# Moving the attention transposes and value products one unit later in a fused attention, MLP and expert kernel

## The chip, the cores and the metric

The kernel runs on one core of a Trainium2 chip. The metric is the device time of one execution in microseconds (us); several runs are given by their median. TensorE is called PE here, VectorE DVE, ScalarE ACT, GpSimd POOL and SyncE SP, as in the profile.

## The reference

Three stages follow one another, all in float32:

```python
# 1. attention: q, k, v are (4, 8, 576, 64); M_prev (4, 8, 64, 64), z_prev (4, 8, 64), beta (8)
scores = np.matmul(q, k.transpose(0, 1, 3, 2)) / np.sqrt(D)        # causal mask, softmax over keys
local = np.matmul(softmax(scores), v)
q_p = phi(q)                                                        # x > 0: x + 1, else exp(x)
mem_out = einsum('bhsd,bhde->bhse', q_p, M_prev) / (einsum('bhsd,bhd->bhs', q_p, z_prev)[..., None] + 1e-06)
x = g * mem_out + (1 - g) * local                                   # g = sigmoid(beta), per head
# 2. MLP on 2304 tokens of 512: w_in (512, 2048), w_out (2048, 512)
x = relu(x @ w_in) ** 2 @ w_out
# 3. one expert of eight for each token, by cosine similarity: w1 (8, 512, 1024), w2 (8, 1024, 512)
out = gate * (relu(x @ w1[e]) @ w2[e])
```

## The kernel before

**Units.** Two heads make a pair; there are 16 pairs, four to each of the four batches. A pair has nine units, in the order `ORDER`: first `(None, 4)`, the last 64 rows of both heads at once, and then a head (0 or 1) and a block r of 128 rows: (0, 3), (1, 3), (0, 0), (1, 0), (0, 2), (1, 2), (0, 1), (1, 1). The main loop of `attention` counts steps `t`; in step `t` the scores of unit `t` are issued, so that pair `p` begins at step `9p`. Within a pair the step is called `i` here (0 to 8).

**A unit's way through the engines.** In its step PE multiplies (`scores`, L437) into a bank of PSUM. One step later DVE adds the mask, copies and finds the row maximum (L441), and ACT takes the exponential (L447). Two steps later, once both heads of a block are there, DVE forms the reciprocal sums (L455, L456) and POOL scales (`scale`): in the first batch a diagonal matrix (L395), in later batches the matrix `A` itself (L398), for both heads together with the second one. `LT = 4` steps after the scores PE transposes (`turn`, L403, or L405 with the diagonal), into two PSUM banks of the tag T. In the step after that ACT copies the transposes out (L575), and `LP = 7` steps after the scores PE multiplies by the values (`values`, L531) and, once a pair, by `M_prev` (L510, L534).

**Preparation of the next pair.** The generator `prep(p + 1)` begins in pair `p` at step `i = START` (3 for the first pair, 2 for the second, 1 afterwards) and takes one stage a step. It transposes k (`tk`, L294) and q (`tq`, L300), splits each into a high and a low part (ACT L295, L301; DVE L296, L302), moves halves with DMAs (`moves`, L290), transposes the 64 last rows of both (`t2`, L324, L325) and splits them too (`tail_hi` on ACT L328, L331; `tail_lo` on DVE L334, L337). It also forms phi(q) (ACT L321, DVE L344, L345), weighs it with z_prev (POOL L348), sums (DVE L353) and normalises (POOL L361); these results are transposed last (`tp`, `t3`). The scores of the next pair's `(None, 4)` read the split tails. `kn` and `qn`, which take k and q, are single buffers.

**Loads.** `load(p + 2)` issues all inputs of a pair on SP's queue: three DMAs each for k, q and v, two for M_prev and one for z_prev, at step `START + 5`.

**The MLP in between.** From step 44 on, `step` gives half a step of the MLP to each step of the loop but `i = REST = 4`: either twelve matmuls of its first layer (L681) or six of its second (L715 to L717). While it has begun only what the finished batches allow, `batches = (t - 8) // 36` sets the limit. Its weights must be split into high and low parts before, and this conversion is spread over steps 5 to 64 (`CONV`: 27 stages by step 43, 51 by step 64). A piece of weights is loaded into one of two `raw` tiles, and passes ACT (L132), DVE (L134 to L139), ACT (L141) and POOL (L143). Two pieces are under way at once (`conversions2`); the next piece's load is issued in the first of the three stages of each round, which is also the stage in which DVE reads the older piece's `raw` tile for the last time (L139).

**Order.** PE runs in the order of the program throughout. Up to step 8 ACT, DVE and POOL do too; later their order, and that of SP's queue at all times, comes from a planner that works with its own estimates of costs and dependencies. Every engine runs its list in order.

Of the kernel before, what the change touches and what calls it, by code (L numbers as in the profile page):

```python
# [14 lines left out]
ALU = mybir.AluOpType  # L15
# [9 lines left out]
NPP = H // 2  # L25
NPAIR = B * NPP
# [22 lines left out]

LT, LP = 4, 7
WT = 2
NA, NAS = 3, 4
XD = 4
# [102 lines left out]
def conversions2(*args):  # L158


    old = iter(())
    new = conversion(*args[:4], 0, *args[4:])
    next(new)
    for n in range(1, 18):
        for k in range(3):
            next(old, None)
            next(new, None)
            if k == 0 and n < 16:
                ahead = conversion(*args[:4], n, *args[4:])
                next(ahead)  # L170
            yield
        old, new = new, ahead if n < 16 else iter(())


def attention(tc, sh, q, k, v, M, z, beta, w_in, w_out, mlp, step):

    nc = tc.nc
    with ExitStack() as ctx:
# [36 lines left out]
        def later(d, eng, f):  # L215
            queue.setdefault((now[0] + d, eng), []).append(f)

        def load(p):
            b, hp = divmod(p, NPP)
            vn = vns[p % 3]  # L220
            zb = st.tile([128, 128], F32, name="zb", tag="zb")
            Mt = Mts[p % 3]
            for src, t in ((k, kn), (q, qn), (v, vn)):
                eng = nc.scalar if p == 0 and src is q else nc.sync
                for h in range(2):
                    eng.dma_start(t[:, 0:4, h * 64:h * 64 + 64],
                                      src[b, 2 * hp + h, 0:512].rearrange("(c p) d -> p c d", p=128))
                eng.dma_start(t[:64, 4].rearrange("p (h d) -> p h d", h=2),
                                  src[b, 2 * hp:2 * hp + 2, 512:576].rearrange("h p d -> p h d"))
            for h in range(2):  # L230
                hs = slice(h * 64, h * 64 + 64)
                nc.sync.dma_start(Mt[hs, hs], M[b, 2 * hp + h])
            nc.sync.dma_start(zb, z[b:b + 1, 2 * hp:2 * hp + 2].rearrange("o h d -> o (h d)").to_broadcast([128, 128]))
            nat[p] = (vn, zb, Mt)

        load(0)
        warm = c.tile([128, 1], F32, name="warm")
        nc.scalar.activation(warm, ident[:, 0:1], AF.Exp)
        g_all = c.tile([128, H], F32, name="g_all")
# [33 lines left out]
        def prep(p):  # L273
# [46 lines left out]

            later(1, "act", lambda: nc.scalar.activation(e, qn, AF.Exp))  # L321
            yield
            t2 = new_T(p, "t2")
            nc.tensor.transpose(t2[:, 0:64], kn[:64, 4], ident[:64, :64])  # L324
            nc.tensor.transpose(t2[:, 64:128], qn[:64, 4], ident[:64, :64])  # L325
# [13 lines left out]

            later(1, "act0", tail_hi)  # L340
            later(1, "dve0", tail_lo)

            def phi():
                nc.vector.tensor_scalar_min(e, e, 1.0)  # L344
                nc.vector.scalar_tensor_tensor(e, qn, 0.0, e, ALU.max, ALU.add)  # L345

            later(1, "dve", phi)
            later(1, "pool", lambda: nc.gpsimd.tensor_tensor(u, e, zb.unsqueeze(1).to_broadcast([128, 5, 128]), ALU.mult))  # L348
            for _ in range(2 if p else 4):
                yield  # L350

            def norm():
# [209 lines left out]
        while t < len(units) + LP + 5 or queue:  # L562
            now[0] = t
            p, i = divmod(t, 9)
            if t == STRICT:
                strict.close()
            if t in BUSY:
                busy(BUSY[t])
            if t == 1:
                load(1)  # L570
            start = START[min(p, 2)]
            if 0 <= p < NPAIR - 1 and i == start:
                gens.append(prep(p + 1))
            for d, x in evacs:
                nc.scalar.copy(d, x)  # L575
            evacs.clear()
            due("act0")
            if before is not None:
                next(before)
            if here is not None:  # L580
                next(here)
            due("dve0")
            if here is not None:
                next(here)
            before, here = here, None
            if t == MIX:
                mix()
            due("act")
            due("dve")
            due("pool")  # L590
            while sh.converted < int(by(CONV, t)):
                next(conv, None)
                sh.converted += 1
            if 0 <= t - LP < len(units):
                values(*units[t - LP])
            if 0 <= p < NPAIR - 2 and i == start + 5:
                load(p + 2)
            if t % 9 != REST:
                step(t)
            for g in list(gens):  # L600
                if next(g, gens) is gens:
                    gens.remove(g)
            if 0 <= t - LT < len(units):
                turn(*units[t - LT])
            if 0 <= t < len(units):
                here = scores(*units[t])
                next(here)
            t += 1
# [743 lines left out]
@with_exitstack  # L1352
def tile_kernel(ctx, tc, q, k, v, M, z, beta, w_in, w_out, emb, tau, w1, w2, out):
    nc = tc.nc
    sh = Shared()
    sh.R = None
    sh.const = ctx.enter_context(tc.tile_pool(name="const", bufs=1))
    big = ctx.enter_context(tc.tile_pool(name="big", bufs=1))
    dr = ctx.enter_context(tc.tile_pool(name="dr", bufs=1, space=DRAM))
    sh.x2p = dr.tile([NT, DM], F32, name="x2p")  # L1360
    sh.x2d = dr.tile([NT, DM], F32, name="x2d")
    sh.end = dr.tile([E, DM], F32, name="end")
    sh.ident = sh.const.tile([128, 128], F32, name="ident")
    make_identity(nc, sh.ident)
    sh.Wh = [[big.tile([128, 1024], F32R, name=f"Wh0_{j}") for j in range(8)]]
    sh.Wl = [[big.tile([128, 1024], F32R, name=f"Wl0_{j}") for j in range(8)]]
    sh.room = ctx.enter_context(tc.tile_pool(name="room", bufs=1))
    sh.x1 = {j: big.tile([128, 4, CH], F32, name=f"x1_{j}") for j in range(NCH - 2)}
    psm = ctx.enter_context(tc.tile_pool(name="psm", bufs=2, space=PSUM))
    with ExitStack() as mctx:  # L1370
        mlp = Mlp(mctx, psm, tc, sh, w1, w2)

        sh.converted, sh.begun = 0, False

        def step(t):


            batches = (t - 8) // (9 * NPP)
            if sh.begun:
                mlp.second()  # L1380
            elif mlp.at < 48 and ((mlp.at + 1) // 8 + 1) * CH <= batches * S and min(6 * mlp.at + 9, 51) <= sh.converted:
                mlp.square = nc.scalar if mlp.at < 16 else nc.vector
                mlp.first()
            else:
                return
            sh.begun = not sh.begun

        with tc.manual_schedule(engines={ENG.PE}):
            attention(tc, sh, q, k, v, M, z, beta, w_in, w_out, mlp, step)
        mlp.later = at_once  # L1390
        mlp.square = nc.scalar
        mlp.psr = sh.psr = ctx.enter_context(tc.tile_pool(name="psr", bufs=1, space=PSUM))
        mlp.room = {NCH - 3: 3, NCH - 2: 7}
        big2 = ctx.enter_context(tc.tile_pool(name="big2", bufs=1, side="right", reuse_waits="tile"))
        sh.Wh.append([big2.tile([128, 1024], F32R, name=f"Wh1_{j}") for j in range(8)])
        sh.Wl.append([big2.tile([128, 1024], F32R, name=f"Wl1_{j}") for j in range(8)])
        with ExitStack() as cctx:
            st = cctx.enter_context(tc.tile_pool(name="cst", bufs=2))
            conv = conversions(nc, st, sh, 1, nc.vector, w_in, w_out)
            done = 0  # L1400
            while mlp.steps[mlp.at][0] == 0:
                mlp.advance()
                done += CONV2
                while done >= 1:
                    next(conv, None)
                    done -= 1
            for _ in conv:
                pass
            for _ in range(mlp.LAG):
                mlp.advance()  # L1410
        mlp.square = nc.scalar
        routing_setup(tc, sh, ctx.enter_context(tc.tile_pool(name="rp", bufs=1, side="right", reuse_waits="tile")))
        sh.R.ps = ctx.enter_context(tc.tile_pool(name="prr", bufs=1, space=PSUM, side="right", reuse_waits="tile"))
        mlp.routing(sh.rpool, mctx.enter_context(tc.tile_pool(name="late", bufs=2, reuse_waits="tile")), emb, tau)
        while mlp.advance():
            pass
        for _ in sh.R.first:
            pass
    gates = tables(ctx, tc, sh)
    next(gates)  # L1420
    experts(tc, sh, gates, w1, w2, out)
# [31 lines left out]
```

## Time and profile before

| | |
|---|---|
| median of 3 runs | 965.38 us (962.93 to 967.06) |
| the profiled execution: its time | 968.15 us |
| the profiled execution: its span | 966.4 us |
| PE busy over the span | 914.8 us |
| pairs 8 to 15 of the attention, each | about 24.2 us |
| end of the attention's loop | about 411 us |

The span runs from the first to the last instruction; the time holds 1.75 us more around it. A pair is measured from the first matmul of its `(None, 4)` scores to that of the next pair. Pair 1 begins at 31.21 us, pair 2 at 55.40, pair 3 at 73.48, pair 4 at 97.88, pair 5 at 118.10, pair 6 at 146.48, pair 7 at 174.56 and pair 8 at 201.22. In a row of a timeline the first number is the start, the second the duration, and a bracket holds the idle time of the engine before it with what ended it.

### The profile page before, as it was taken

The numbers are of one execution on the slowest core, as the hardware profiler recorded it, in microseconds if no ns is written. First come the engines' busy times: TensorE is split into PE (matmuls) and PEld (weight loads), VectorE is DVE, ScalarE is ACT, GpSimd is POOL, SyncE is SP. The second block draws the span as 40 slices with busy tenths as digits, with TensorE's granted clock in tenths as the row PEclk, the third lists the DMA queues.
The fourth block names the chain that finished last, engine by engine and source line by source line (L and its number), as shares of the span: only waits on it lengthen the run. The fifth ranks groups of instructions, "written<-read, shape, count | busy, mean of one in ns | idle before, by whom it ended". The sixth has DMA issues, their size and how long they took to land.

```text
span 966.4 us, 19224 instructions
## 1 busy us (share of the span) xinstructions
PE 914.8 (95%) x6271; PEld 792.3 (82%) x6271; DVE 604.4 (63%) x1745; ACT 526.2 (54%) x1355; POOL 281.5 (29%) x353
## 2 busy tenths in 40 slices
PE   7987888899999999999999999999999999999993
PEld 6765766688888888899888888888899899989983
DVE  4886677656666665488616778889772535353661
ACT  3676677677666766577645555655421424242440
POOL 4453555533333443100211111333310311111111
PEclk8999999899999999999999999999999999999997
DMA  7676555454444440155220111521160634353521
GB/s 162 141 181 154 141 157 134 102 124 95 119 97 119 95 99 1 66 154 167 89 73 23 55 63 69 198 66 45 34 219 14 198 104 155 114 168 94 173 82 34
DMA packets 107081, 105.79 MB, mean 109 GB/s; under 512 B 66096, under 2 KB 76336, under 8 KB 106945
## 3 DMA queue, kind: packets, MB, share of 16 engines
q1 hardware_dynamic: 101200, 90.17, 33.6%
q0 software_dynamic: 4544, 13.67, 4.5%
q8 instruction: 65, 1.06, 0.5%
q14 instruction: 72, 0.58, 0.2%
q10 hardware_dynamic: 1200, 0.30, 0.2%
HBM read 70.80 MB, written 14.70 MB: 88 GB/s over the span
## 4 chain that ended last, share of the span: by engine, by line
PE 74%; issue 5%; DVE 3%; POOL 1%; ACT 0%; POOLq 0%; DVEq 0%
PE ps L681 20%; PE psh L1248 11%; PE y L715 7%; PE y L717 6%; PE y L716 6%; PE psy L1266 3%; PE psy L1264 3%; PE psy L1265 3%; PE xo L531 3%; PE ps L437 3%; PE pt L403 3%; DVE x L818 1%; PE xo L510 1%; PE pst L964 1%; POOL out_dram L1329 0%
## 5 line engine op out<-in xcount | busy, mean ns | idle before, releaser
L681 PE MATMUL ps<-xh,Wh 128*128 128x256 f32 x416 | 120.1, 289 | 0.0
L681 PE MATMUL ps<-xl,Wh 128*128 128x256 f32 x416 | 118.2, 284 | 1.0 <-DVE xl L655 1.0
L681 PE MATMUL ps<-xh,Wl 128*128 128x256 f32 x416 | 118.1, 284 | 0.0
L447 ACT ACTIVATE A<-A,nm 128x576 f32<-128x576 f32 (+2 forms) x144 | 84.4, 586 | 59.7 <-DVE nm L441 40.5
L715 PE MATMUL y<-Wh,gh 128*128 128x512 f32 x288 | 115.3, 400 | 0.0
L717 PE MATMUL y<-Wh,gl 128*128 128x512 f32 x288 | 113.7, 395 | 0.1
L716 PE MATMUL y<-Wl,gh 128*128 128x512 f32 x288 | 113.4, 394 | 0.0
L398 POOL TENSOR_SCALAR A<-A,sm,g 128x512 f32<-128x512 f32 (+4 forms) x108 | 74.1, 694 | 119.4 <-DVE sm L456 77.7
L1250 ACT ACTIVATE hh<-psh 128x512 fp32r<-128x512 f32 x44 | 26.4, 599 | 147.3 <-PE psh L1248 76.4
L1248 PE MATMUL psh<-xTh,Wh 128*128 128x256 f32 x352 | 100.1, 284 | 2.0 <-issue 1.3
L691 DVE TENSOR_TENSOR gl<-r,gh 128x256 fp32r<-128x256 f32 x144 | 73.8, 514 | 42.3 <-ACT gh L690 38.4
L1248 PE MATMUL psh<-xTh,Wl 128*128 128x256 f32 x352 | 99.5, 283 | 0.2 <-DVE Wl L111 0.2
L1248 PE MATMUL psh<-xTl,Wh 128*128 128x256 f32 x352 | 99.3, 282 | 0.0
L685 ACT ACTIVATE r<-ps 128x256 f32<-128x256 f32 x144 | 54.6, 379 | 74.2 <-PE ps L681 64.7
L441 DVE CUSTOM_DVE_ANT_0 A<-ps,mask 128x256 f32<-128x256 f32 (+4 forms) x160 | 75.6, 479 | 26.6 <-PE ps L437 24.7
L1251 DVE SCALAR_TENSOR_TENSOR hl<-psh,hh 128x512 fp32r<-128x512 f32 x44 | 30.4, 690 | 94.9 <-ACTq L1238 38.1
L681 PEld LDWEIGHTS ps<-xh,Wh 128*128 128x128 f32 x416 | 79.8, 192 | 4.7 <-issue 1.9
L681 PEld LDWEIGHTS ps<-xl,Wh 128*128 128x128 f32 x416 | 79.9, 192 | 3.8 <-DVE xl L655 1.2
L681 PEld LDWEIGHTS ps<-xh,Wl 128*128 128x128 f32 x416 | 79.9, 192 | 0.0
L690 ACT CAST gh<-r 128x256 fp32r<-128x256 f32 x144 | 58.4, 405 | 38.3 <-PE y L716 35.4
L1248 PEld LDWEIGHTS psh<-xTh,Wh 128*128 128x128 f32 x352 | 66.9, 190 | 4.0 <-issue 2.1
L1248 PEld LDWEIGHTS psh<-xTl,Wh 128*128 128x128 f32 x352 | 66.8, 190 | 0.7
(328 smaller groups left out, 2416.2 us busy)
## 6 DMA issues: line engine op xcount, KB each, us to landing
x<-in_moe_w_dram SPq DMA_DIRECT2D x48, 512.0 KB, 8.8
raw<-in_moe_w_in_dram SPq DMA_DIRECT2D x16, 512.0 KB, 4.7
raw<-in_moe_w_out_dram SPq DMA_DIRECT2D x16, 512.0 KB, 3.8
ks<-hk SPq DMA_DIRECT2D x60, 128.0 KB, 2.5
x2d<-x SPq DMA_DIRECT2D x18, 256.0 KB, 2.0
kn<-in_k_dram SPq DMA_DIRECT2D x32, 128.0 KB, 4.2
vn<-in_v_dram SPq DMA_DIRECT2D x32, 128.0 KB, 3.6
x2p<-x SPq DMA_DIRECT2D x16, 256.0 KB, 2.0
```

What stands on the lines that cost most here:

```text
L398: nc.gpsimd.tensor_scalar(A, A, a, b, ALU.mult, ALU.mult)
L441: nc.vector.tensor_tensor_reduce(A[:, a:a + w], tiles[j][:, :w], mask[:, end - w:end], -1.0, 3e38, ALU.add, ALU.min, nm[:, j:j + 1])
L447: nc.scalar.activation(A[:, :n], A[:, :n], AF.Exp, bias=nm[:, 0:1], scale=-1.0, accum_out=sm[:, i:i + 1])
L681: nc.tensor.matmul(ps[:, :CH], a, b, start=n == 0, stop=n == len(ops) - 1)
L685: self.later(1, "act", lambda: nc.scalar.activation(r, ps[:, :CH], AF.Relu))
L690: self.later(3, "act", lambda: nc.scalar.copy(gh, r))
L691: self.later(3, "dve", lambda: nc.vector.tensor_tensor(gl, r, gh.bitcast(F32), ALU.subtract))
L715: nc.tensor.matmul(y, gh[:, sl], wh, start=first, stop=False)
L716: nc.tensor.matmul(y, gh[:, sl], wl, start=False, stop=False)
L717: nc.tensor.matmul(y, gl[:, sl], wh, start=False, stop=last)
L1248: nc.tensor.matmul(ps[:, a], w[kc][:, sl], x[:, kc], start=kc + j == 0, stop=kc + j == 5)
L1251: nc.vector.scalar_tensor_tensor(hl, ps, 0.0, hh.bitcast(F32), ALU.max, ALU.subtract)
```

## The change

`LT` goes from 4 to 5 and `LP` from 7 to 8. The rest of the edit moves work around that: the MLP's limit counts batches one step later; in `prep`, for every pair but the first, the tail's transposes `t2` come one step later and phi(q)'s stages keep their steps; `load(p + 2)` is split, so that k, q and z_prev are issued after the step's `prep` (which now holds `t2`) and v and M_prev in a step of their own, after that step's `values`; and the load of the next `raw` tile is issued in the second stage of a conversion round instead of the first.

```diff
-LT, LP = 4, 7
+LT, LP = 5, 8
...
-            if k == 0 and n < 16:
+            if k == 1 and n < 16:
                 ahead = conversion(*args[:4], n, *args[4:])
                 next(ahead)
...
         def load(p):
             b, hp = divmod(p, NPP)
+            fetch(p, (k, kn), (q, qn))
             zb = st.tile([128, 128], F32, name="zb", tag="zb")
+            nc.sync.dma_start(zb, z[b:b + 1, 2 * hp:2 * hp + 2].rearrange("o h d -> o (h d)").to_broadcast([128, 128]))
+            nat[p] = (vns[p % 3], zb, Mts[p % 3])
+
+        def load_values(p):
+            b, hp = divmod(p, NPP)
+            fetch(p, (v, vns[p % 3]))
+            for h in range(2):
+                hs = slice(h * 64, h * 64 + 64)
+                nc.sync.dma_start(Mts[p % 3][hs, hs], M[b, 2 * hp + h])
...
             later(1, "act", lambda: nc.scalar.activation(e, qn, AF.Exp))
             yield
+            def weigh():
+                later(1, "dve", phi)
+                later(1, "pool", lambda: nc.gpsimd.tensor_tensor(u, e, zb.unsqueeze(1).to_broadcast([128, 5, 128]), ALU.mult))
+
+            if p:
+                weigh()
+                yield
             t2 = new_T(p, "t2")
...
-            for _ in range(2 if p else 4):
+            if p == 0:
+                weigh()
+            for _ in range(1 if p else 4):
                 yield
...
-            if 0 <= p < NPAIR - 2 and i == start + 5:
-                load(p + 2)
+            if 0 <= p < NPAIR - 2 and i == min(start + 6, 8):
+                load_values(p + 2)
             if t % 9 != REST:
                 step(t)
             for g in list(gens):
                 if next(g, gens) is gens:
                     gens.remove(g)
+            if 0 <= p < NPAIR - 2 and i == start + 5:
+                load(p + 2)
             if 0 <= t - LT < len(units):
                 turn(*units[t - LT])
...
-            batches = (t - 8) // (9 * NPP)
+            batches = (t - 9) // (9 * NPP)
```

## Rows read from the trace of the kernel before

**Rows 1.** The page: PE's busy time, and the granted clock in 40 slices.
```profile
PE 914.8 (95%) x6271; PEld 792.3 (82%) x6271; DVE 604.4 (63%) x1745; ACT 526.2 (54%) x1355; POOL 281.5 (29%) x353
...
PEclk8999999899999999999999999999999999999997
```

**Rows 2.** Busy time by stretches: pairs 1, 3, 5, 6, 10, and the attention's end.
```profile
core 0: us, PE busy (x) PEld busy (x) DVE busy (x) ACT busy (x) POOL busy (x), PEclk, DMA share, GB/s
...
31.21:55.40 24.19, 18.75 (x139) 14.98 (x137) 23.52 (x66) 16.50 (x47) 13.78 (x16) 0.90 0.61 148
...
73.48:97.88 24.40, 17.97 (x138) 14.11 (x137) 15.82 (x52) 14.86 (x40) 9.36 (x14) 0.93 0.62 151
...
118.10:146.48 28.38, 25.02 (x180) 20.42 (x178) 18.81 (x57) 21.09 (x59) 16.69 (x16) 0.94 0.53 141
146.48:174.56 28.08, 20.59 (x150) 15.31 (x148) 24.55 (x66) 19.44 (x54) 14.82 (x17) 0.98 0.58 139
...
249.56:273.73 24.17, 24.17 (x186) 20.19 (x184) 14.65 (x49) 15.76 (x49) 9.07 (x11) 1.00 0.44 96
...
394.00:411.00 17.00, 17.00 (x115) 13.92 (x114) 7.12 (x19) 8.57 (x23) 0.98 (x2) 1.00 0.19 63
```

**Rows 3.** PE's timeline, 45 to 180 us: rows with long idle time before them.
```profile
54.10 1.65 PE L405 MATMUL pt<-x,A 128*128 128x128 f32 x6 [2.44 <-POOL x L395]
...
72.79 0.94 PE L405 MATMUL pt<-x,A 128*128 128x128 f32 x6 [1.36 <-POOL x L395]
...
80.57 0.63 PE L368 MATMUL tp<-ident,e 128*128 128x128 f32 x4 [3.55 <-POOL x L395]
...
97.19 0.94 PE L405 MATMUL pt<-x,A 128*128 128x128 f32 x6 [2.58 <-POOL x L395]
...
125.18 0.88 PE L300 MATMUL tq<-ident,qn 128*128 128x128 f32 x4 [2.17 <-ACT ATa L575]
...
174.00 0.90 PE L403 MATMUL pt<-ident,A 128*128 128x128 f32 x3 [3.72 <-POOL A L398]
```

**Rows 4.** Stretches right behind three of these waits, columns as in group 2.
```profile
97.90:101.30 3.40, 3.40 (x20) 3.40 (x18) 2.18 (x9) 1.35 (x3) 2.30 (x4) 0.54 0.34 119
125.10:128.90 3.80, 3.72 (x17) 3.53 (x18) 3.80 (x10) 2.44 (x7) 2.27 (x3) 0.55 0.26 79
174.00:180.00 6.00, 6.00 (x28) 6.00 (x29) 4.29 (x13) 2.14 (x6) 5.46 (x7) 0.50 0.06 14
```

**Rows 5.** Timeline of all engines before pair 1: the tail of k and q.
```profile
28.65 0.27 PE L324 MATMUL t<-ident,kn 64*128 64x64 f32 x1
...
30.29 0.44 ACT L331 ACTIVATE qbh<-t 64x64 fp32r<-64x64 f32 x2
...
31.11 0.21 DVE L337 SCALAR_TENSOR_TENSOR qbl<-t,qbh 64x64 fp32r<-64x64 f32 x1
...
31.21 0.39 PE L437 MATMUL ps<-hk,qbh 128*128 128x320 f32 x1
```

**Rows 6.** DVE's timeline, around the waits.
```profile
79.75 0.67 DVE L296 TENSOR_TENSOR kl<-tk,hk 128x512 fp32r<-128x512 f32 x1
...
99.12 0.82 DVE L353 TENSOR_REDUCE nr<-u 128x10 f32<-128x640 f32 x1 [2.20 <-POOL u L348]
...
172.33 0.41 DVE L441 CUSTOM_DVE_ANT_0 A<-ps,mask 128x256 f32<-128x256 f32 x1
```

**Rows 7.** POOL's timeline before the wait at 97 us.
```profile
96.69 0.88 POOL L395 TENSOR_SCALAR x<-ident,sm,g 128x128 f32<-128x128 f32 x2
```

**Rows 8.** One kind of DVE instruction beside POOL and, later, without it.
```profile
45.16 1.28 POOL L143 TENSOR_TENSOR Wl<-wt,Wh 128x512 fp32r<-128x512 f32 x1 [1.43 <-ACT Wh L141]
45.19 1.80 DVE L137 SCALAR_TENSOR_TENSOR wt<-raw,wt 128x512 int32<-128x512 int32 x1
...
57.57 0.69 DVE L137 SCALAR_TENSOR_TENSOR wt<-raw,wt 128x512 int32<-128x512 int32 x1
```

**Rows 9.** ACT's timeline: its wait for a raw tile.
```profile
43.24 0.68 ACT L132 ACTIVATE wt<-raw 128x512 f32<-128x512 f32 x1 [1.54 <-DMA raw<-in_moe_w_in_dram]
```

**Rows 10.** SP's waits to 400 us: total, times, longest.
```profile
SPq L124 <- DVE wt L139: 11.7, 3, 7.1
```

**Rows 11.** The page's DMA issues: count, KB each, median us to landing.
```profile
raw<-in_moe_w_in_dram SPq DMA_DIRECT2D x16, 512.0 KB, 4.7
```

More of the change, by code (lines that the diff above doesn't have):

```diff
@@ L219, in load, with fetch @@
             b, hp = divmod(p, NPP)
-            vn = vns[p % 3]
+            fetch(p, (k, kn), (q, qn))
             zb = st.tile([128, 128], F32, name="zb", tag="zb")
-            Mt = Mts[p % 3]
-            for src, t in ((k, kn), (q, qn), (v, vn)):
+            nc.sync.dma_start(zb, z[b:b + 1, 2 * hp:2 * hp + 2].rearrange("o h d -> o (h d)").to_broadcast([128, 128]))
[6 more added lines that the diff above has]
+                nc.sync.dma_start(Mts[p % 3][hs, hs], M[b, 2 * hp + h])
+        def fetch(p, *pairs):
+            b, hp = divmod(p, NPP)
+            for src, t in pairs:
                 eng = nc.scalar if p == 0 and src is q else nc.sync
@@ L229, in load @@
                                   src[b, 2 * hp:2 * hp + 2, 512:576].rearrange("h p d -> p h d"))
[L230 to L234, printed above, removed]
         load(0)
+        load_values(0)
         warm = c.tile([128, 1], F32, name="warm")
@@ L322, in prep, with phi @@
             yield
+            def phi():
+                nc.vector.tensor_scalar_min(e, e, 1.0)
+                nc.vector.scalar_tensor_tensor(e, qn, 0.0, e, ALU.max, ALU.add)
+            def weigh():
[4 more added lines that the diff above has]
+                yield
             t2 = new_T(p, "t2")
@@ L341, in prep @@
             later(1, "dve0", tail_lo)
[L343 to L348, printed above, removed]
-            for _ in range(2 if p else 4):
+            if p == 0:
+                weigh()
+            for _ in range(1 if p else 4):
                 yield
@@ L570, in attention @@
                 load(1)
+                load_values(1)
             start = START[min(p, 2)]
```

## Prediction, made before the changed kernel was run

> **What bounds the kernel now.** I read the page first, then the busy time pair by pair, then PE's timeline with its waits, then the other engines' timelines at those waits. The page says that PE is busy 914.8 us of 966.4, and its clock is below full almost only in the first seven of forty slices and at the end [rows 1]. So what is to be gained at once lies before about 180 us. The view by pairs shows it: pair 10 takes 24.17 us with PE busy all of it at full clock, while pairs 1, 3, 5 and 6 hold 5.4, 6.4, 3.4 and 7.5 us in which PE does nothing, at clocks of 0.90 to 0.98 [rows 2]. From pair 8 on the attention is PE's work and nothing else, and so is its end, 17.00 of 17.00 us [rows 2]; an edit that only moves waits does nothing there, but time saved before is kept, since PE takes up the same work earlier.
>
> In PE's timeline four of the six long waits stand in front of the same thing, a group of three transposes (x6 with the diagonal, two matmuls for each; x3 without): unit (0, 2), which is turned at the first step of the next pair, before that pair's first scores. They last 2.44, 1.36, 2.58 and 3.72 us, together 10.10 [rows 3]. Head 0's scale waits for head 1's sums, one unit later, so only one step lies between the scale and the transposes. The other two long waits are of another kind: 3.55 us before tp and 2.17 us before tq [rows 3]. tp needs the PSUM bank of tk, and DVE's copy of it, at 79.75 for 0.67 us, ends at 80.42, just before PE goes on at 80.57 [rows 6]; the releaser named, POOL, is a near miss. After long waits PE runs for a while at the lower level, 1.2 GHz instead of 2.4: 0.54 over 3.4 us, 0.55 over 3.8 and 0.50 over 6.0 [rows 4]. At (1 - clock) times the stretch these cost 1.6, 1.7 and 3.0 us.
>
> **The change part by part.** The sum is made against the profiled execution, 968.15 us, which is 2.8 above the median of 965.38.
>
> *Transposes a step later.* Ahead of the turn of (0, 2) PE can now issue the next pair's first scores (0.9 us at full clock) and tk's four transposes, with two short transposes of (1, 0): some 1.8 us of work, an estimate from pair 2's start in the same timeline. What becomes of each wait:
> - 97.19: 2.58 falls to about 0.8, and the low clock behind it, 1.6, may go too: at most 3.4. But DVE does not follow PE here: its queue stands 2.20 us for POOL until 99.12 [rows 6], and POOL ran the scales only from 96.69 [rows 7]. PE would come to the next thing that DVE owes it earlier, and wait there. I take 0.7 (bounds 0 and 3.4).
> - 72.79: 1.36 goes, but the wait at 80.57 is set by DVE and grows instead. I take 0.3 (bounds 0 and 1.36).
> - 54.10: pair 1 is DVE's, 23.52 us busy of 24.19 [rows 2]. I take 0.5 (bounds 0 and 2.44 with 1.6 of clock, as behind 97.19).
> - 174.00: what follows is bounded by PSUM for the scores: the copy at 172.33 for 0.41 us frees a bank at 172.75 [rows 6], so PE moves on 1.25 us earlier with no transposes in the way. After 180 us nothing gives it back, and with a shorter idle time the 3.0 us of low clock can go: 1.2 + 2.8 = 4.0 (bounds 1.2 and 3.72 + 3.0 = 6.7).
> - 125.18 and the smaller waits of pairs 5 and 6: before, step i = 4 takes three transposing banks of the two there are (t3 and both of (None, 4)), and now no step takes more than two. tq itself is not helped. Idle time there is 3.4 + 7.5 us less the 3.72 just counted, so 7.2. I take 2.0 (bounds 0 and 7.2 + 1.7).
>
> Together 0.7 + 0.3 + 0.5 + 4.0 + 2.0 = 7.5.
>
> *Values a step later* keep three steps to their transposes, and the queue behind them is the same. The loop runs one step longer, and its end is full of MLP work [rows 2]: nothing, and if that cover failed, one half step of the MLP, about 1.4 us. The limit of batches moves by a step with it: in steps 48 to 64 the MLP waits for converted weights anyway, so that its order catches up. Nothing.
>
> *Tail a step later.* Before pair 1 t2 was transposed at 28.65, ACT had split it from 30.29 on, DVE from 31.11, and the scores that need it began at 31.21 [rows 5]: no slack at all. Now t2 stands in the last step of pair 0, about 1 us later, with ACT's and DVE's parts due in the step that needs them. I charge 1.5 (bounds 0 and 2.5, the 2.46 us from t2 to DVE's part in full). Before pair 2 one step is left, and from pair 3 on two: nothing.
>
> *Loads split.* Twelve DMAs a pair as before, in two groups. k's issue now also waits for t2 in the same step, and behind it on SP's queue stand q, z_prev and the next raw tile; k is wanted four steps later. v and M_prev have more than a pair. z_prev goes ahead of them. Nothing; uncovered, a late k would stop PE at tk.
>
> *Raw tiles a stage later.* The load was issued in the very stage in which DVE frees the tile, so SP stood for DVE's last read: 11.7 us in three waits for one kind of piece alone, 7.1 the longest, with the moves of k and q queued behind [rows 10]. A stage later the tile is free when SP comes. But the piece also lands later by up to a stage: 38 steps hold 27 stages, so 1.4 steps, of some 2.7 us in pairs 1 and 3, or 3.8 us. It takes 4.7 us to land [rows 11], and ACT has waited for one once, 1.54 us [rows 9]. I take nothing (bounds: a gain of 3 us, about a quarter of SP's waits, and the loss of the third rival).
>
> Net: 7.5 - 1.5 = 6.0; 968.15 - 6.0 = 962.1, and against the median, 2.8 lower, 959.3: **959 us**, 0.7% faster.
>
> **Two rules weighed.** DVE's instruction of line 137 takes 0.69 us alone and 1.80 when POOL begins at the same moment, POOL's own 1.28 being within its usual length [rows 8]. The Trainium skill, SBUF — State Buffer, section SBUF: two separate sides, says that the two share a pair of ports as an exclusive lock, so that the loser stands for the winner's whole instruction. By that rule a new order costs wherever it makes them meet; it has a rival of its own.
>
> In pair 10 PE is busy 24.17 of 24.17 us, but loading weights only 20.19, or 84% [rows 2]. The Trainium skill, Perfetto Trace Analysis, section Identifying the Most-Contended Engine, says that matmul busy time does not tell how near PE is to its limit and that weight loading does. The row gives no gain in pairs 8 to 15; by the rule there may be some, and that too is a rival.
>
> **The rivals.**
> 1. *DVE and POOL set the pace, no change.* For it: pair 1, the wait at 80.57, DVE's own stand for POOL at 99.12. PE's waits then move one instruction on. Against it: at 174.00 DVE has freed the bank and PE stands for POOL alone. All but 1.2 of the gain is lost, the tail costs 1.5: 968.4, or 966 at the median.
> 2. *All of it counts.* The four waits fall by 1.8, 1.36, 1.8 and 1.25, clock is regained at three of them (1.6 + 1.6 + 3.0), and pairs 5 and 6 give 2.5: 14.9 less 1.5 is 13.4, so 952. For it: the clock is lost only behind the long waits, none behind the 1.36. Against it: DVE as above.
> 3. *Slower: ACT waits for raw tiles.* In-order ACT stands before L132, and behind it the copies out of PSUM, and so PE. It decides once a load lands more than about 2 us later than before. Of the some nine pieces of steps 9 to 45, three would wait, with the 3.8 us less 2 us of slack each, 5.4, the tail 1.5 and a clock loss of 1.6, against 3 kept: 968.15 + 5.5, or 971. Against it: one wait of 1.54 in all so far.
> 4. *Ports.* Six more meetings at 1.80 - 0.69 = 1.1 us on DVE, in pairs where DVE is behind: 6.6 against 4 kept: 968.
> 5. *Hidden slack in pairs 8 to 15.* If a twentieth of 24.2 us came free in eight pairs, 9.7 on top of the forecast: 949. The starts of matmuls there follow each other without a gap, so this is nearly excluded.
>
> **Chances.** Forecast 0.40 (955 to 963), rival 1 0.22, rival 2 0.20, rival 3 0.11, rival 4 0.04, rival 5 0.03. About 0.5%, or 4.8 us, is what a measurement can tell from no change: the line is 960.5. Of the forecast 0.28 lies below it and 0.12 above; faster 0.28 + 0.20 + 0.03 = 0.51, same 0.12 + 0.22 + 0.03 = 0.37, slower 0.11 + 0.01 = 0.12. The range of 949 to 967 leaves out rival 3, most of rival 4 and the far ends of rivals 2 and 5, together about 0.19; the likeliest case by itself is 955 to 963.
>
> **What the profile after would show.** Right: no wait over 1 us before the three transposes of (0, 2), nothing of the low clock from 174 to 180, pair 8 beginning some 6 us earlier than 201.22, SP no longer standing for L139, and pairs of 24.2 us from then on. A wait for qbh or qbl before pair 1's first scores of about 1.5 us would confirm the tail's price. Wrong: the waits for tp, tk or scores' banks grow by what the others lose (rival 1); ACT's idle time before L132 grows (rival 3); the pairs after the eighth get shorter (rival 5); or the planner puts DVE's or POOL's work in another order altogether, which no row of the kernel before can show.

## The result, and the profile after

The changed kernel takes 977.18 us (median of 4 runs, 975.00 to 980.49) beside 965.27 for the kernel before (4 runs, 962.93 to 967.06). The ratio is 1.0128, with a 95% interval of 1.0090 to 1.0165: 1.3% slower, where 0.7% faster was forecast and 967 was the range's upper end.

The profiled execution after took 976.26 us with a span of 974.5, against 968.15 and 966.4. So these two differ by 8.1 us, and the medians by 11.9: the profiled one of before lies 2.9 above its median, that of after 0.9 below. The traces are compared here, and at the end of this section what they leave out.

First the page of the changed kernel: PE's busy time and the granted clock in 40 slices.

```profile
PE 917.0 (94%) x6271; PEld 793.1 (81%) x6271; DVE 609.0 (62%) x1745; ACT 525.9 (54%) x1355; POOL 288.2 (30%) x353
...
PEclk8898979999999999999999999999999999999997
```

The instruction counts are those of [rows 1], so nothing was added or left out. Busy time on PE grew by 2.2 us and the span by 8.1. The digit of the granted clock is lower than before in the second, fourth and sixth slice and higher in the eighth.

Next the busy time by stretches of the changed kernel: pairs 1, 3, 5, 6 and 10, and 9.4 us of pair 5. The columns are those of [rows 2].

```profile
31.03:54.15 23.12, 19.25 (x136) 15.65 (x136) 20.75 (x56) 14.93 (x40) 12.29 (x15) 0.85 0.52 123
71.58:94.00 22.42, 18.52 (x138) 14.82 (x137) 16.64 (x54) 15.09 (x41) 11.85 (x15) 0.85 0.63 152
116.95:149.34 32.39, 25.95 (x173) 20.54 (x172) 22.04 (x59) 20.34 (x55) 17.59 (x18) 0.84 0.50 122
149.34:177.19 27.85, 22.32 (x155) 17.55 (x154) 24.14 (x60) 18.92 (x54) 15.29 (x16) 0.94 0.55 138
252.54:277.30 24.76, 24.43 (x186) 20.39 (x184) 14.34 (x50) 15.68 (x47) 8.86 (x11) 1.00 0.42 94
126.60:136.00 9.40, 8.89 (x32) 5.82 (x34) 5.51 (x17) 7.43 (x20) 2.96 (x3) 0.51 0.81 197
```

Beside [rows 2], pairs 1 and 3 are shorter (23.12 and 22.42 for 24.19 and 24.40), pair 5 is 4.0 us longer, and pair 10, which was full, now holds 0.33 us without PE and takes 24.76 for 24.17. From the starts of the pairs the 8.1 us split up as follows (positive: the changed kernel is later):

| point | lag | what was added on the way |
|---|---|---|
| start of pair 4 | -3.9 | pairs 1 to 3 |
| start of pair 5 | -1.15 | +2.7 in pair 4 |
| start of pair 6 | +2.9 | +4.0 in pair 5 |
| start of pair 8 | +1.5 | -0.2 and -1.15 in pairs 6 and 7 |
| start of pair 15 | +5.8 | +4.4 in pairs 8 to 14, some 0.6 each |
| end of the span | +8.1 | +2.3: pair 15 (0.6), a wait of 1.09 us for the routing at 484 us, and 0.6 that was not followed up (the loop has one more step) |

So there are two main losses: 1.5 us by pair 8, where 6 us were to have been gained, and then a steady 0.6 us in each pair of the stretch that was full. Of the 14.1 us between the forecast (6.0 earlier) and these traces (8.1 later), 7.5 arise before pair 8, 4.9 in pairs 8 to 15 and 1.7 behind them.

**Where the waits went.** PE's timeline of the changed kernel, rows with long idle time ahead of them; the releaser stands in the bracket.

```profile
33.21 0.45 PE L451 MATMUL ps<-hk,qbl 128*128 128x320 f32 x1 [1.77 <-DVE qbl L356]
...
47.10 2.04 PE L419 MATMUL pt<-x,A 128*128 128x128 f32 x8 [2.10 <-ACT AT L590]
...
79.43 1.12 PE L382 MATMUL tp<-ident,e 128*128 128x128 f32 x4 [3.65 <-POOL e L375]
...
100.55 0.68 PE L419 MATMUL pt<-x,A 128*128 128x128 f32 x4 [2.25 <-DVE kl L303]
...
126.58 1.12 PE L307 MATMUL tq<-ident,qn 128*128 128x128 f32 x4 [5.93 <-DVE kl L303]
...
173.51 0.87 PE L417 MATMUL pt<-ident,A 128*128 128x128 f32 x3 [2.46 <-DVE qbl L356]
```

Not one of them stands for the scale of (0, 2), for which PE waited four times in [rows 3]. They stand for DVE's parts of k and q (`kl`, `qbl`), for POOL's `e` and for copies on ACT. At 100.55, 126.58 and 173.51 PE does not read the results `kl` or `qbl`: it needs the bank of PSUM that they are read out of. How much idle time there is in all from 31 to 200 us is said by one row of each trace, before and then after:

```profile
31.00:200.00 169.00, 142.17 (x1036) 114.46 (x1035) 127.01 (x386) 118.52 (x329) 85.57 (x99) 0.93 0.59 144
```

```profile
31.00:200.00 169.00, 142.09 (x1024) 113.75 (x1024) 131.52 (x380) 116.43 (x323) 90.68 (x99) 0.91 0.60 144
```

PE idles for 26.83 us before and for 26.91 after. The waits changed their places and releasers, and their sum stayed. The clock over the stretch fell from 0.93 to 0.91; one of the new waits is as long as 5.93 us, and PE ran at 1.2 GHz for 9.4 us behind it (0.51 in the stretch from 126.60).

A stretch of fixed length need not hold the same work in both. The stretch from the start of pair 1 to that of pair 8 holds all of pairs 1 to 7, again before and then after:

```profile
31.21:201.22 170.01, 143.18 (x1041) 115.20 (x1040) 127.22 (x386) 119.48 (x333) 85.57 (x99) 0.93 0.59 144
31.03:202.70 171.67, 144.78 (x1042) 116.15 (x1042) 132.40 (x383) 118.27 (x330) 90.65 (x99) 0.91 0.59 144
```

The idle time is 26.83 and 26.89 us. So the 1.66 us by which the stretch is longer are busy time (1.60 of them), at a lower clock.

What stands ahead of kl at the wait of 5.93 us is seen in DVE's timeline of the changed kernel:

```profile
121.01 0.82 DVE L367 TENSOR_REDUCE nr<-u 128x10 f32<-128x640 f32 x1 [1.92 <-POOL u L337]
...
122.60 0.94 DVE L135 TENSOR_SCALAR wt<-wt 128x512 int32<-128x512 int32 x1
123.57 1.62 DVE L137 SCALAR_TENSOR_TENSOR wt<-raw,wt 128x512 int32<-128x512 int32 x1
125.23 0.69 DVE L139 SCALAR_TENSOR_TENSOR wt<-raw,wt 128x512 int32<-128x512 int32 x1
125.84 0.69 DVE L303 TENSOR_TENSOR kl<-tk,hk 128x512 fp32r<-128x512 f32 x1
```

DVE first stands 1.92 us for POOL and then takes one piece of weights through four conversion instructions (L134 is among the lines left out) before it comes to kl. ACT, in order too, stands meanwhile for the same piece, with the copy of a transposes' bank behind it. PE had come to tq at 120.65 us, and DVE reached kl at 125.84. Of the four instructions L137 took 1.62 us, with POOL's L375 running (from 123.23, for 1.42), against 0.69 alone in [rows 8].

Before, PE came to tq at 123.01 and waited 2.17 us [rows 3], although `kl` came later there, at 127.22. There tq took the other bank, which ACT's copy of ATa empties, and that copy stood ahead of L141 in ACT's list. In the changed kernel it stands behind L141. ACT's rows, two before and two after:

```profile
124.64 0.48 ACT L575 COPY ATa<-pt 128x384 f32<-128x384 f32 x1
126.67 0.62 ACT L141 CAST Wh<-wt 128x512 fp32r<-128x512 f32 x1 [1.24 <-DVE wt L139]
...
125.95 0.62 ACT L141 CAST Wh<-wt 128x512 fp32r<-128x512 f32 x1 [4.92 <-DVE wt L139]
126.48 0.47 ACT L590 COPY ATa<-pt 128x384 f32<-128x384 f32 x1
```

So DVE was not later at this place than before. In the planner's new order both banks come free only behind the piece of weights.

**What the traces leave out.** The runs' mean granted clocks are 0.966 to 0.975 after and 0.976 to 0.983 for the kernel before, whose profiled execution has 0.976. So the trace of before is of an execution with a lower clock than usual, and as far as the clocks tell, the remaining 3.8 us between 8.1 and 11.9 belong there; no trace shows a usual run of before.

One trace also shows one execution. Three of the kernels below (the changed kernel with the pause on step 5, alone, with the gap in steps 45 to 47 and with dummies in step 47) have the same program up to step 44, and yet pair 1 begins at 30.88, 31.82 and 35.53 us in their traces and pair 5 at 116.25, 118.56 and 118.86. A difference of 2 or 3 us between two traces before pair 8 is therefore a reading of these executions and not shown for the usual run. The 0.6 us of the steady pairs come back in every one of them.

### The profile page after: what moved, and what is told of

The parts are those of the page before. It is cut to its first block, busy times and chain, and to the rows that moved or that the text cites. A ratio compares the mean times of both kernels' runs of the same rounds, so it can differ in the third digit from the quotient of the medians.

```text
span 974.5 us, 19225 instructions
## 1 busy us (share of the span) xinstructions
PE 917.0 (94%) x6271; PEld 793.1 (81%) x6271; DVE 609.0 (62%) x1745; ACT 525.9 (54%) x1355; POOL 288.2 (30%) x353
## 4 chain that ended last, share of the span: by engine, by line
PE 72%; DVE 9%; issue 7%; DMA 5%; ACT 5%; POOL 2%; SPq 0%; ACTq 0%; POOLq 0%; DVEq 0%
PE ps L698 16%; PE psh L1265 10%; PE y L732 6%; PE y L734 6%; PE y L733 6%; PE xo L545 4%; PE ps L451 4%; PE psy L1283 3%; PE psy L1281 3%; PE psy L1282 3%; PE pt L417 3%; PE pt L419 2%; DVE A L455 1%; PE xo L524 1%; ACT A L461 1%
## 5 line engine op out<-in xcount | busy, mean ns | idle before, releaser
L412 POOL TENSOR_SCALAR A<-A,sm,g 128x512 f32<-128x512 f32 (+4 forms) x108 | 77.7, 726 | 144.9 <-DVE sm L470 35.5
L461 ACT ACTIVATE A<-A,nm 128x576 f32<-128x576 f32 (+2 forms) x144 | 84.9, 590 | 56.3 <-DVE nm L455 35.9
L708 DVE TENSOR_TENSOR gl<-r,gh 128x256 fp32r<-128x256 f32 x144 | 68.0, 473 | 66.7 <-ACT gh L707 65.7
L1281 PE MATMUL psy<-Wh,hh 128*128 128x512 f32 x168 | 67.0, 399 | 0.1
```

The lines of the kernel that those rows point to most:

```text
L412: nc.gpsimd.tensor_scalar(A, A, a, b, ALU.mult, ALU.mult)
L461: nc.scalar.activation(A[:, :n], A[:, :n], AF.Exp, bias=nm[:, 0:1], scale=-1.0, accum_out=sm[:, i:i + 1])
L708: self.later(3, "dve", lambda: nc.vector.tensor_tensor(gl, r, gh.bitcast(F32), ALU.subtract))
L1281: nc.tensor.matmul(y[h], xh, wh, start=g + a == 0, stop=False)
```

## The experiments

Theory A says that the 0.6 us in each steady pair come from the pause: `REST = 4` keeps the MLP out of step i = 4, where with `LP = 7` PE had the large values product of unit (1, 2) instead, and with `LP = 8` that product is in step 5. Theory B lays the loss before pair 8 to the raw tile's load a stage later. Theory C lays the steady loss to the longer lead itself, by the two transposing banks. Theory D (the wait for tq in pair 5 comes of the conversion ahead of `kl`) was added with the second group of runs, theory E (the low clock behind long waits is what they cost) with the third. All times are medians, and each ratio is to the kernel before on the same chip (964.23, 965.38 and 965.67 us).

First the steps in question, in the timeline of PE. The kernel before, pair 10, the end of step 3 and step 4:

```profile
257.83 0.28 PE L437 MATMUL ps<-kl,qz 128*128 128x256 f32 x1
257.94 1.02 PE L510 MATMUL xo<-pT,Mt 128*128 128x512 f32 x2
258.89 1.74 PE L531 MATMUL xo<-ATa,vn 128*64 128x256 f32 x16
260.56 0.27 PE L372 MATMUL t<-ident,e 64*128 64x64 f32 x1
260.76 0.76 PE L403 MATMUL pt<-ident,A 128*128 128x128 f32 x5
```

The changed kernel, the same steps:

```profile
260.71 0.28 PE L451 MATMUL ps<-kl,qz 128*128 128x256 f32 x1
260.92 0.27 PE L386 MATMUL t<-ident,e 64*128 64x64 f32 x1
261.52 0.63 PE L417 MATMUL pt<-ident,A 128*128 128x128 f32 x4 [0.33 <-ACT pT L387]
...
262.22 1.02 PE L524 MATMUL xo<-pT,Mt 128*128 128x512 f32 x2
263.17 1.74 PE L545 MATMUL xo<-ATa,vn 128*64 128x256 f32 x16
```

Before, 2.6 us of values product lie between the scores of step 3 and t3. After, nothing does: step 4 has neither MLP nor values, and PE comes to the next transposes before ACT has emptied their bank. From t3's start to theirs it is 0.60 us, for 0.20 before. That is 0.40 of the 0.59 us by which this pair is longer; 0.09 more stand just ahead of t3, and 0.09 ahead of the product of (None, 4).

**The changed kernel with the pause on step 5.**

```diff
-REST = 4
+REST = 5
```

> The changed kernel with the MLP's pause moved from step i = 4 to i = 5. Theory A (the pause stayed on a step from which the large value products have moved away, so PE runs ahead there and waits for ACT's copy of tp or t3 in every pair): pairs 8 to 15 go back from 24.76 us to 24.2, and the kernel to about 971 to 973 us. Theory B (the raw tiles' later load, or a new order on DVE, costs the time in pairs 4 and 5): pairs 8 to 15 may shorten but pairs 4 and 5 keep their 6.7 us; below 971 would speak against B as the larger part. Theory C (the longer lead itself costs, by PSUM banks held longer): pairs 8 to 15 keep 24.7 us, 977.

972.23 us, ratio 1.0096 (1.0078 to 1.0114), 3 us under the changed kernel by the ratios and 5 by the medians. One steady pair, then the stretch from 31 to 200 us:

```profile
249.82:274.16 24.34, 24.34 (x186) 20.27 (x184) 13.76 (x50) 15.55 (x47) 8.92 (x11) 1.00 0.43 96
31.00:200.00 169.00, 141.67 (x1035) 114.25 (x1036) 129.64 (x381) 117.44 (x326) 89.53 (x99) 0.92 0.60 145
```

The idle time in the pair is gone and the pair takes 24.34 us, nearly as before (24.17). The first stretch is not healed: 27.33 us of idle time.

**The kernel before with the pause on step 5**, the same edit as a control.

> The kernel before with the MLP's pause moved from step i = 4 to i = 5, the counterpart of the move that helped the changed kernel. Theory A (the pause has to stand in the step with the large values product of unit (1, 2), which with LP = 7 is i = 4): the paused step loses its cover, pairs 8 to 15 grow from 24.17 to 24.4 to 24.8 us with a short wait in each, and the time is 967 to 971. Rival (step 5 is simply a better place for the pause in both kernels): pairs of 24.17 or less and 962 to 965.

971.89 us, ratio 1.0064 (1.0046 to 1.0082). Pair 10 of it:

```profile
248.84:273.78 24.94, 24.46 (x185) 20.25 (x184) 13.56 (x49) 15.67 (x47) 9.07 (x11) 1.00 0.42 93
```

and what PE waits for in each such pair:

```profile
263.13 0.27 PE L324 MATMUL t<-ident,kn 64*128 64x64 f32 x1 [0.48 <-ACT AT L575]
```

The pairs grew by 0.77 us each, and this and the time are a little more than was expected. The same edit mends one kernel and harms the other, so neither step 4 nor step 5 is better for the pause in itself: it must be the step with the large product. That is theory A, in both directions.

**Only the raw tile's load taken back.**

```diff
-            if k == 1 and n < 16:
+            if k == 0 and n < 16:
```

> The changed kernel with the raw tiles' load back in the first stage of a conversion round. Theory B: pairs 4 and 5 give back most of their 6.7 us, about 970 to 973 us. Theories A and C: nothing, 976 to 978, and pairs 8 to 15 stay at 24.7 us, since no conversion runs there.

978.08 us, ratio 1.0148 (1.0126 to 1.0170): nothing regained. In its trace pairs 4 and 5 give back 1.2 of the 6.7 us (54.1 for 55.3 in all), and the steady pairs take 24.76 as before this edit. So theory B, which wanted most of the 6.7 back, is wrong.

**Only the leads taken back**, with the tail a step later and the split loads kept.

```diff
-LT, LP = 5, 8
+LT, LP = 4, 7
...
-            batches = (t - 9) // (9 * NPP)
+            batches = (t - 8) // (9 * NPP)
```

> The changed kernel with the leads and the limit of batches back (4, 7), so the rest of the change alone. Theories A and C: pairs 8 to 15 at 24.2 us, 964 to 968. Theory B: pairs 4 and 5 keep their loss, 969 to 973.

973.01 us, ratio 1.0100 (1.0083 to 1.0117). Its steady pairs are longer still, 25.1 us, with this wait in each:

```profile
268.71 0.80 PE L545 MATMUL xo<-AT,vn 128*64 128x64 f32 x20 [0.91 <-ACT ATa L590]
```

So the later tail is no free edit: the product of (None, 4), whose result takes a bank of T as well, comes with `LP = 7` in the step right behind t2's, and a bank is then missing. The expectation of theories A and C was missed, and theory B's range was just left (973.01 for 969 to 973) without its condition: pairs 4 and 5 take 49.9 us, for 55.3 in the changed kernel and 48.6 before. So the loss there goes with the leads. In pair 5 tq waits 2.92 us, and ACT's copy stands ahead of L141 again (123.34 and 126.26). The gain over the changed kernel comes before pair 8, which begins at 199.41.

**Only the leads, on the kernel before** (`LT, LP = 5, 8`, `t - 9`). With the old load of v a step ahead of the last values product, some products take a later pair's v.

> The kernel before with nothing but the two leads (5 and 8) and the limit of batches. Theory A: pairs 8 to 15 take 24.7 us, as in the changed kernel; with what pairs 1 to 3 gained there, 967 to 971. Theory B: pairs 4 and 5 as before, so 963 to 968 if it holds alone. Theory C: as in the changed kernel, 975 to 978.

1030.87 us, ratio 1.0693 (1.0675 to 1.0710). Since x differs, the routing gives out more blocks (416 matmuls of each kind in L1248, 352 before), so the time as a whole can't be compared. Within the attention the pairs take 26.2 us, more than in any other kernel here, and PE waits in each for ACT's copies of AT and pT (some 0.7 and 0.4 us): the leads need the other edits.

**The transposes' lead kept, that of the values taken back.**

```diff
-LT, LP = 5, 8
+LT, LP = 5, 7
...
-            batches = (t - 9) // (9 * NPP)
+            batches = (t - 8) // (9 * NPP)
```

> The changed kernel with LP back at 7 and the MLP's limit back at t - 8, LT = 5 kept: only the transposes come a step later, the values keep their step and with it the cover of the paused step. Theory A: pairs 8 to 15 of 24.2 to 24.3 us and 970 to 973, some 5 us under the changed kernel, the rest being lost before 180 us as in it. Rival C (the longer lead of the transposes itself costs, by PSUM banks): pairs stay at 24.7 and the time at 975 to 979.

977.39 us, ratio 1.0115 (1.0083 to 1.0148), the steady pairs 25.2 to 25.3. Theory A's expectation of 24.2 was missed, and the wait shows where:

```profile
251.59 0.80 PE L545 MATMUL xo<-AT,vn 128*64 128x64 f32 x20 [1.06 <-ACT ATa L590]
```

What the product reads, AT, had been copied by 247.23. It starts once ACT has copied ATa out of a bank of T, at 251.54, so what it lacked is a bank for its result, in the step behind t2's as in the run with both leads back. So the later tail and `LP = 7` don't go together, with `LT` at 4 or at 5. The run therefore doesn't tell A from C; the two runs of the pause do.

**The pause on step 5 and the old order of the tail** (t2 ahead of phi's stages again, for every pair).

```diff
-            if p:
-                weigh()
-                yield
             t2 = new_T(p, "t2")
...
-            if p == 0:
-                weigh()
-            for _ in range(1 if p else 4):
+            weigh()
+            for _ in range(2 if p else 4):
```

> The changed kernel with the pause on i = 5 and the order of t2 and phi(q) as before (t2 a step earlier for every pair but the first). If the tail's price of about 1.5 us at pair 1 is real and is kept to the end: pair 1 begins 1 to 1.5 us earlier than 30.88 and the time is 970.5 to 971.3. If DVE and POOL swallow it in pairs 1 to 3: pair 4 begins where it did and the time is 972 to 973. If the third transposing group in one step costs in the steady pairs: pairs of 24.5 or more and over 974.

976.17 us, ratio 1.0111 (1.0082 to 1.0139). Pair 1 begins at 30.92 and pair 4 at 93.36, for 30.88 and 93.30 without this edit: what the tail costs at pair 1 isn't kept. In the steady pairs, now 25.06 us, it costs:

```profile
265.37 0.33 PE L413 MATMUL pt<-ident,A 128*128 128x128 f32 x1 [0.68 <-ACT AT L586]
```

With `LT = 5`, t2's old step is one with three transposing banks (its own and both of (None, 4)); the later tail is what the longer lead of the transposes needs, as the longer lead of the values is what the later tail needs.

**The pause on step 5 and no conversion in steps 45 to 47.**

```diff
-CONV = [(5, 0), (43, 27), (64, 51)]
+CONV = [(5, 0), (43, 27), (44, 28), (47, 28), (64, 51)]
```

> The changed kernel with the pause on i = 5 and, beyond that, no stage of the conversion in steps 45 to 47 (the stages up to 64 are made up evenly after them). Theory D (in pair 5 PE stands 5.93 us for tq because DVE's conversion stages run ahead of kl, and ACT's copies behind one of them): that wait falls under 2.5 us, the low clock behind it goes, pair 6 begins 2 to 4 us earlier against pair 4's start, and the time is 967.5 to 970.5. Rival 1 of the prediction (DVE and POOL set the pace over all of the pairs 1 to 6, so the wait moves on): pair 7 begins where it did and the time is 971.5 or more.

973.94 us, ratio 1.0083 (1.0056 to 1.0111); the wait for tq is 5.94 us as before, and pair 7 begins at 174.05 for 173.87, as rival 1 had it. The edit missed its aim: the four instructions ahead of kl are stages of steps up to 44, which DVE reaches only when PE is at step 47. That DVE is that far behind is the answer that the run gives.

**The same gap, earlier**, on the changed kernel with the pause on step 5, and on the kernel before.

```diff
-CONV = [(5, 0), (43, 27), (64, 51)]
+CONV = [(5, 0), (40, 25), (46, 25), (64, 51)]
```

> The changed kernel with the pause on i = 5 and the conversion held at 25 stages in steps 40 to 46, made up evenly by step 64, so that the four DVE instructions of one piece (L134 to L139) no longer stand ahead of kl in pair 5; an earlier gap in steps 45 to 47 began too late for that, since DVE was still at the stages of step 44. Theory D (kl behind the conversion makes the 5.93 us and the low clock behind it): the wait for tq falls to 2.5 us or less, pair 6 begins 2.5 to 4.5 us earlier after pair 5 than in the run it is made from, and the time is 967 to 970. Rival 1 of the prediction (DVE and POOL set the pace, the wait moves on): pair 7 begins within 1 us of where it did and the time is 971.5 or more.

> The kernel before with the same gap in the conversion. Theory D: its wait of 2.17 us for tq at 125 us goes and 1.7 us of low clock with it, so 961 to 963. Rival 1: the stages come later and stand before something else, 964.5 to 967.

On the changed kernel 968.93 us, ratio 1.0043 (1.0024 to 1.0062). Pairs 4 and 5 by stretches, and the whole to 200 us:

```profile
31.00:200.00 169.00, 142.23 (x1054) 114.43 (x1054) 133.38 (x390) 118.94 (x331) 90.99 (x101) 0.94 0.60 145
93.23:119.51 26.28, 18.21 (x135) 14.51 (x134) 19.16 (x56) 15.31 (x45) 12.77 (x14) 0.87 0.47 109
119.51:144.08 24.57, 21.89 (x174) 17.99 (x172) 16.56 (x50) 19.16 (x54) 14.86 (x16) 1.00 0.69 174
```

Pair 5 no longer waits for kl, keeps its full clock and shrinks from 30.76 to 24.57 us. But pair 4 grows from 22.95 to 26.28, since its own tq now waits 7.51 us for kl. Of the two pairs' 53.7 us 2.9 are gained, and pair 8 begins 2.8 earlier (198.36). From the start of pair 1 to that of pair 8 this kernel takes 167.68 us for 170.27; 2.03 of the difference are busy time (140.91 for 142.94), at a clock of 0.94 for 0.92, and 0.56 idle time (26.77 for 27.33). The ratios, 1.0043 and 1.0096, say the same of the whole. On the kernel before the gap does nothing, 966.22 us, ratio 1.0010 (0.9988 to 1.0032): its wait for tq grew from 2.17 to 3.86 us where it was to go. On the changed kernel theory D's expectation is met (967 to 970) and that of rival 1 is not: pair 7 begins 3.1 us earlier, not within 1. But the wait has moved on to another pair, as rival 1 has it, and on the kernel before rival 1's expectation is the one that is met (964.5 to 967). So neither holds alone.

**Work for the idle PE.** Dummy transposes (matmuls into a bank that nobody reads) at the start of a step, on the changed kernel with the pause on step 5, then on the kernel before.

```diff
-STRICT, BUSY = 9, {-5: 14, 0: 12, 2: 6}
+STRICT, BUSY = 9, {-5: 14, 0: 12, 2: 6, 47: 45}
```

> The changed kernel with the pause on i = 5 and 45 dummy transposes (some 5 us of PE at full clock, into a bank that nobody reads) at the start of step 47, so that PE isn't idle while it waits for tq in pair 5. They change no dependency. If the clock is what the idle time costs (theory E): no stretch at the lower level from 126 to 136 us, pair 5 shorter by 3 to 4 us, and the time 968 to 970. If the idle time itself is the cost and the clock little: pair 5 as long as it was or longer, and 971.5 to 974.

971.16 us, ratio 1.0055 (1.0034 to 1.0076), between the two expectations. The wait for tq fell to 1.01, a new one of 4.67 us stood before tp, and pair 5 is longer (33.87 us); yet pairs 6 and 7 are so much shorter that pair 8 begins 81.9 us after pair 5, not 84.9.

```diff
-STRICT, BUSY = 9, {-5: 14, 0: 12, 2: 6}
+STRICT, BUSY = 9, {-5: 14, 0: 12, 2: 6, 18: 18, 27: 20, 47: 16, 63: 30}
```

> The kernel before with dummy transposes at the start of steps 18, 27, 47 and 63 (18, 20, 16 and 30 of them, 2 to 3.3 us), ahead of the long waits of 2.44, 2.58, 2.17 and 3.72 us. Theory E (the clock is what long waits cost behind themselves, 1.6 + 1.7 + 3.0 us in the trace of before): 959 to 962. If the dummies push real work on PE back, or the clock falls all the same: 965 to 968.

961.02 us, ratio 0.9950 (0.9933 to 0.9967): faster than both kernels, with 84 matmuls more. PE's timeline at the wait of 174 us, and the stretch to 200 us:

```profile
169.33 5.02 PE L559 MATMUL w<-ident 128*128 128x128 f32 x30
174.18 0.49 PE L403 MATMUL pt<-ident,A 128*128 128x128 f32 x3
174.43 0.40 PE L437 MATMUL ps<-hk,qbh 128*128 128x320 f32 x1
```

```profile
31.00:200.00 169.00, 147.54 (x1136) 119.94 (x1135) 130.42 (x390) 119.07 (x334) 87.92 (x101) 0.97 0.59 146
```

The transposes of (0, 2) begin as late as in [rows 3], at 174.18 for 174.00, but what follows runs at full speed. Three stretches of the same trace, the dummies' first half, their second, and what comes behind:

```profile
169.33:172.00 2.67, 2.67 (x14) 2.67 (x14) 2.67 (x9) 2.26 (x9) 2.29 (x4) 0.50 0.19 45
172.00:174.18 2.18, 2.18 (x19) 2.18 (x18) 0.77 (x4) 0.00 (x0) 2.18 (x3) 0.87 0.18 41
174.18:180.00 5.82, 5.82 (x43) 5.42 (x42) 3.94 (x14) 4.61 (x13) 2.22 (x4) 1.00 0.22 49
```

The dummies run through the slow stretch (0.50, then 0.87), so that real work begins at 1.00 where [rows 4] had 0.50; pair 7 takes 24.16 us, 2.5 less than before. Over the whole stretch the clock is 0.97 for 0.93. At this wait theory E holds: it was paid for a second time behind itself.

Over pairs 1 to 7 together the gain is smaller than the clock's part. They take 167.59 us for 170.01. Dummies (11.40) and idle time (21.46) come to 32.86 us, for 26.83 of idle time before, which leaves 134.73 us of PE for the real work; before, it took 143.18. Pairs 3, 4 and 7 became 1.9, 1.2 and 2.5 us shorter, but pairs 5 and 6 2.2 and 1.3 longer. The expectation also had one wait in the wrong step: step 27 is that of the wait of 1.36 us, while the wait of 2.58 stands at step 36, had no dummies, and is 4.08 us long in this run. And of the 4.6 us between the profiled executions (963.55 and 968.15) 2.6 are there at pair 8; the other 2.0 arise behind the attention, where the edit changes nothing.

## Why the prediction was wrong

Two steps failed: the price of the later values, and the gain from the waits.

**The first step that failed** is "values a step later ... nothing", together with the sentence it rests on, that from pair 8 on an edit that only moves waits does nothing. PE was full there, but full because each step's work covered ACT's copies; moving 2.6 us of product out of the paused step took that cover away. The loss is 0.6 us in each of pairs 8 to 15, 4.9 in all, and the two runs of the pause show the cause: 24.76 to 24.34 us in the one kernel, 24.17 to 24.94 in the other. The prediction asked what covers the loop's extra step, and not what the product itself covered. Of the 0.59 us, 0.49 lie around t3 in the paused step (0.33 of it shown as idle time). Another 0.09, ahead of the product of (None, 4), is there with the pause on step 5 too and is about half of the 0.17 that this run keeps; its cause was not looked for.

The Trainium skill, Perfetto Trace Analysis, section Optimization Strategy, says that the same gap repeating on an engine that should be full can mean too few buffers for the next tile. The gap of 0.33 us agrees: it is a wait for one of the two T banks. Here the order of the work removed it, without a further bank.

**The second step that failed** is the gain from the waits before 180 us, forecast at 7.5 us. That the four waits for (0, 2) would end was right: none is left. What they would be worth was wrong: no term's lower bound lay below zero. Pairs 5 to 7, for which 6.0 of it stood in the sum (4.0 and 2.0), lost 2.6 instead: tq waited longer, and at the place of the wait of 174 us DVE was late with `qbl`, 2.46 us. Pair 4, which had no term, lost 2.7. Pairs 1 to 3, where 1.5 of gain and 1.5 of loss stood against each other, gained 3.9. The sum of idle time stayed, 26.83 and 26.91 us, as rival 1 would have it (DVE and POOL set the pace). It was given 0.22, and its price of 966 left out that waits which move can gather into a longer one, and what the clock then takes. In pair 5 that came about where the planner's new order has both banks come free behind a piece of weights; a new order, of DVE's or POOL's work, was among the signs of being wrong that the prediction named.

From 31 to 200 us the idle time is between 26.55 and 28.82 us in all eleven kernels that leave the result as it is and have no further dummies; the lowest is that with `LP` back at 7, the highest that with both leads back. That DVE and POOL are what keeps it there is argued and not shown: no run made either of them faster, and in pair 5 it was the order on ACT and DVE that counted.

The reading behind the bound of 180 us was off by a slice: the page's clock digits are below 9 in the first, the eighth and the last slice, and a 9 stands for 90% or more. The bound itself holds by the rows of the pairs.

**The tail** was priced at 1.5, and pair 1's first scores waited 0.19 and 1.77 us for qbh and qbl, 1.96 in all. But by pair 4 nothing of it was left, as the run with the old order shows.

**The loads and the raw tiles** at nothing: for the raw tiles this was right, by the run with the old stage. The split loads were not tried by themselves, but from 31 us to the end of the attention's loop PE waits for no DMA in the changed kernel's trace. SP went on standing for L139 none the less (10.9 and 6.1 us in two waits each for the two kinds of piece), which the prediction had thought would end. ACT waits for no raw tile at all, so rival 3, the only slower case, had no part in this. Rival 4 (the shared ports) was not tried by itself; one such meeting stands in the wait of pair 5 (L137, 1.62 us). Rival 5's sign was wrong: the steady pairs had no slack to give, but cover to lose.

## What to carry to other kernels

An engine that is busy without a gap still depends on the order of its work: before a large instruction is moved, look at what it hides in the step that it leaves, and move pauses along with it. Where a wait is taken away, count the idle time of the whole stretch and not the wait: here it stayed within 2.3 us over eleven kernels, and what changed was how it was cut up. Then the length of each piece matters, and dummy work in a wait that can't be avoided may be worth more than an attempt to move it. One trace of each kernel is little to go by where executions of the same program differ by as much as the edit.

## What the hardware showed that was not expected

A wait of 5.93 us left PE at 1.2 GHz (0.51) for the next 9.4 us, in which it was busy for 8.89; one of 1.56 us at 161.74 left the clock at 1.00. Transposes that nobody reads, in the place of a wait of 3.72, brought it back to 1.00 before the work that counts. The Trainium skill, TensorE: Matmul & The Clock Gate, section HAM oscillation — how this bites in real kernels, tells of such waits in a kernel whose PE waits for DMAs, each followed by a stretch at the lower clock; the runs here agree for the longer waits on other engines.
